# Seven products of halves for the last three spans of an expert layer

## The chip, the cores and the metric

The kernel runs on one core of a Trainium2 chip. The engines named are TensorE (PE, with its weight loads shown as PEld), VectorE (DVE), ScalarE (ACT), GpSimd (POOL) and SyncE (SP, which here only issues DMAs). The metric is the device time of one execution in microseconds. Three runs of the kernel before gave 257.63, 256.58 and 257.5 us, a median of 257.5.

## The reference

The work is block-causal attention (8 batches, 8 heads, 576 positions, 64 columns a head, blocks of 64), whose output becomes the input `x` (4608 tokens, 512 columns) of a layer with two parallel first matrices:

```python
attn = softmax(where(block_i >= block_j, q @ k.T / sqrt(64), -1e9))
x = (attn @ v).transpose(0, 2, 1, 3).reshape(4608, 512)
g = np.maximum(x @ w1, x @ w2)      # w1, w2: 512 x 1024
out = g @ w_out                     # w_out: 1024 x 512, out in fp32
```

## The kernel before

The kernel uses max(a, b) = b + relu(a - b). It forms d = w1 - w2 (`d_sb`) and M = w2 @ w_out (`m_sb`) once. Then h = relu(x @ d) is kept in a tile called `g`, and y = x @ M + h @ w_out. So y has an inner length of 512 + 1024 = 1536, that is 12 chunks of 128: four from `xT` against `m_sb` and eight from `g` against `wo_sb`. All of these are bf16; PSUM and the output are fp32.

The tokens are cut into ten spans (lines 70 to 73 of the kernel): 256, 320, then 512 each, and 448 for the last one. A span starts at token t0, and where t0 is not a multiple of 128 the 64 columns that are left over (`carry`) are copied by POOL from the `g` tile of the span before (L235), so that y always works on whole tiles of 128 tokens. From span 2 on each has four such tiles.

For a span, `h_unit(i, f)` makes one of eight blocks of 128 hidden columns: four matmuls with `d_sb` as the stationary operand and up to 512 tokens as the moving one (L243), and then a relu by VectorE from PSUM into `g` (L248). `y_unit(i, s)` makes one tile of 128 tokens by 512 columns: twelve matmuls 512 wide (L285), a copy by VectorE into a `y` tile (L290), and a store from SP's queue (L291). The last tile of all, `y_last` (L294 on), is cut into pieces of 256, 128 and 128 columns. Their copies are by ScalarE, VectorE and ScalarE (L305), and the last piece is stored from ScalarE's queue (L306).

Each unit is a generator that issues one matmul a step. `plan()` puts the units into a list, in order, each with the number of tokens that must be done before it may start, and a cost. `fill(n)` takes steps of the first unit in the list that may start, and the attention code calls it between its own matmuls, so that PE always has something to do. Attention works on pairs of heads (32 pairs, two a group): scores into PSUM (L399, L417), exp by ScalarE (L423), masks by POOL (L428), then the matmul of the attention values (L507) two pairs later, with a reciprocal and a multiply by VectorE (L513, L514) into `xp`. `xp` becomes columns of `xT` by a DMA transpose (L525), or, for the last group, by 18 transposes on PE and two copies by VectorE (L545 to L551). Within the group loop `pool_work(p)` issues POOL's casts and loads after each pair.

The order on each engine is the order in which the program is written out (a manual schedule); nothing is reordered. Tiles come from pools with few buffers: `ps_m` has four PSUM banks, shared by h, y, the attention values and the transposes; `y` has four SBUF tiles; `w1raw` has four, used only while d is made; `bT_sb` is used only while M is made; `qkn` holds cast q and k.

Since the last batch's tokens count as done only when its last group has been transposed, spans 8 and 9, and what is left of span 7, come after attention:

```python
    x_out(NG - 1)
    done_tokens[0] = old
    fill(NY)
    done_tokens[0] = NTOK
    fill(len(units) * NFF * 12)
```

Of the kernel before, what the change touches and what calls it, by code (L numbers as in the profile page):

```python
# [8 lines left out]
FP32 = mybir.dt.float32  # L9
BF16 = mybir.dt.bfloat16  # L10
AF = mybir.ActivationFunctionType
# [3 lines left out]
def kernel(  # L15
# [10 lines left out]
    nc = tc.nc  # L26

    B, H, S, D = q.shape
    P = 128
# [3 lines left out]
    d_model = H * D  # L33
# [3 lines left out]
    NTOK = B * S  # L37
# [33 lines left out]
    spans = [(0, QCUT), (QCUT, S - QCUT)]  # L71
    spans += [(t0, min(SPAN, NTOK - t0)) for t0 in range(S, NTOK, SPAN)]
    NSPAN = len(spans)


    carry = [t0 % P for t0, _ in spans]
    tiles = [(carry[i] + w) // P for i, (_, w) in enumerate(spans)]

# [5 lines left out]
    wraw = ctx.enter_context(tc.tile_pool(name="wraw", bufs=4))  # L84
    qkn = ctx.enter_context(tc.tile_pool(name="qkn", bufs=2))
    g_pool = ctx.enter_context(tc.tile_pool(name="g", bufs=2))
    y_pool = ctx.enter_context(tc.tile_pool(name="y", bufs=4))
    ps_s = ctx.enter_context(tc.tile_pool(name="ps_s", bufs=2, space=bass.MemoryType.PSUM))
    ps_m = ctx.enter_context(tc.tile_pool(name="ps_m", bufs=4, space=bass.MemoryType.PSUM))

# [9 lines left out]
    xT = ring.tile([P, NDM, NTOK + BLK], BF16, name="xT")  # L100
    d_sb = wpool.tile([P, NDM, d_ff], BF16, name="d_sb")
    bT_sb = wpool.tile([P, NFF, d_model], BF16, name="bT_sb")
    m_sb = wpool.tile([P, NDM, d_model], BF16, name="m_sb")
    wo_sb = wpool.tile([P, NFF, d_model], BF16, name="wo_sb")
# [5 lines left out]
    dve, pool, act = nc.vector.tensor_copy, nc.gpsimd.tensor_copy, nc.scalar.copy  # L110
# [51 lines left out]
    def load_v(b, c):  # L162
        rows = min(P, S - c * P)
        nc.gpsimd.dma_start(  # L164
            out=vv_r[b % NV][P - rows:, c, :, :D],
            in_=v[b, :, c * P:c * P + rows, :].rearrange("h p d -> p h d"),
        )
# [7 lines left out]
    for j in range(d_ff // WB):  # L175
        row, n = (1, j) if j < 3 else (3, 0)
        t0 = 3 * S - 3 * BLK + n * NDM * WB
# [21 lines left out]
    dve, pool, act = nc.vector.tensor_copy, nc.gpsimd.tensor_copy, nc.scalar.copy  # L199
# [28 lines left out]
    g_tiles = {}  # L228

    def h_unit(i, f):  # L230
        if f == 0:
            g_tiles[i] = g_pool.tile([P, NFF, SPAN + BLK], BF16, name="g")
            if carry[i]:
                end = carry[i - 1] + spans[i - 1][1]
                nc.gpsimd.tensor_copy(  # L235
                    out=g_tiles[i][:, :, :carry[i]],
                    in_=g_tiles[i - 1][:, :, end - carry[i]:end])
        g = g_tiles[i]
        t0, w = spans[i]
        m = carry[i]  # L240
        pt = ps_m.tile([P, SPAN], FP32, name="ps_h", tag="m")
        for c in range(NDM):
            nc.tensor.matmul(  # L243
                pt[:, :w], d_sb[:, c, f * P:(f + 1) * P], xT[:, c, t0:t0 + w],
                start=(c == 0), stop=(c == NDM - 1),
            )
            if c == NDM - 1:
                nc.vector.tensor_scalar_max(g[:, f, m:m + w], pt[:, :w], 0.0)  # L248
            yield

    def bT_unit(j):
        pt = ps_m.tile([P, 2, NDM, P], BF16, name="ps_bT", tag="m")
        for i in range(2):
            for c in range(NDM):
                nc.tensor.transpose(pt[:, i, c, :], w2_sb[j][:, c, i * P:(i + 1) * P], ident[:])
                if i == 1 and c == NDM - 1:
                    (act if j % 2 else dve)(
                        out=bT_sb[:, 2 * j:2 * j + 2, :],
                        in_=pt.rearrange("p i c d -> p i (c d)"))
                yield  # L260
# [19 lines left out]
    def y_unit(i, s):  # L280
        t0 = spans[i][0] - carry[i] + s * P
        py = ps_m.tile([P, d_model], FP32, name="ps_y", tag="m")
        terms = y_terms(i, s)
        for n, (lhs, rhs) in enumerate(terms):
            nc.tensor.matmul(  # L285
                py[:], lhs, rhs, start=(n == 0), stop=(n == len(terms) - 1),
            )
            if n == len(terms) - 1:
                y = y_pool.tile([P, d_model], FP32, name="y")
                nc.vector.tensor_copy(out=y[:], in_=py[:])  # L290
                nc.sync.dma_start(out=out[t0:t0 + P, :], in_=y[:])  # L291
            yield

    def y_last(i, s):  # L294
        t0 = spans[i][0] - carry[i] + s * P
        for m, w, copy, queue in ((0, 256, act, SP), (256, P, dve, SP), (384, P, act, ACT)):
            py = ps_m.tile([P, w], FP32, name="ps_y", tag="m")
            terms = y_terms(i, s)
            for n, (lhs, rhs) in enumerate(terms):
                nc.tensor.matmul(  # L300
                    py[:], lhs, rhs[:, m:m + w], start=(n == 0), stop=(n == len(terms) - 1),
                )
                if n == len(terms) - 1:
                    y = y_pool.tile([P, d_model], FP32, name="y")
                    copy(out=y[:, :w], in_=py[:])  # L305
                    queue.dma_start(out=out[t0:t0 + P, m:m + w], in_=y[:, :w])  # L306
                yield


    units = []  # L310
    NY = NDM + NFF

    def plan():
        def h(i, f):
            t0, w = spans[i]
            units.append((h_unit(i, f), t0 + w, w / SPAN, NDM))

        def y(i, s, last=False):
            t0, w = spans[i]
            if last:  # L320
                units.append((y_last(i, s), t0 + w, 0.333, 3 * NY))
            else:
                units.append((y_unit(i, s), t0 + w, 1.0, NY))

        for i in range(NSPAN):
            for f in range(NFF):
                h(i, f)
                if i == 0 and f % 2:
                    units.append((bT_unit(f // 2), 0, 0.25, 2 * NDM))
                if i > 2 and f % 2 == 0 and f // 2 < tiles[i - 1]:  # L330
                    y(i - 1, f // 2)
            if i == 1:
                for n in range(2 * NDM):
                    units.append((m_unit(n // NDM, n % NDM), 0, 0.5, NFF))
                for j in range(2):
                    for s in range(tiles[j]):
                        y(j, s)
        n = tiles[-1]
        for s in range(n):
            y(NSPAN - 1, s, s == n - 1)  # L340

    plan()
    todo = [[n, u, need, cost] for u, need, cost, n in units]
# [225 lines left out]
    def pool_work(s):  # L569
        g, i = divmod(s, 2)  # L570
        if s == 4:
            load_qk(4, (SP, SP), gated=True)
        elif s == 5:
            load_qk(5, (SP, SP), gated=True)
            cast("q", 4, ((pool, 0, RPP),))
            cast("k", 4, ((pool, 0, RPP),))
        else:
            if i == 1 and g + 3 < NG:
                load_qk(g + 3, (SP, SP), gated=True)
            if i == 1 and g + 2 < NG:  # L580
                cast("q", g + 2, ((pool, 0, RPP),))
                cast("k", g + 2, ((pool, 0, RPP),))
            nb, j = divmod(s + 2, HP)
            if nb < B:
                for c in ((0, 1), (2, 3), (4,), ())[j]:
                    load_v(nb, c)
            for nm in "qk":
                if i == 1 and g + 3 < NG and by_dma(nm, g + 3):
                    load_blocks(nm, g + 3)
# [112 lines left out]
    n = fill_of(GPB)  # L702
# [10 lines left out]
    for g in range(GPB + 1, NG):  # L713
        a, b = 2 * g, 2 * g + 1
        old = done_tokens[0]
        if x_due:
            x_out(x_due.pop())
        n, new = fill_of(g), done_tokens[0]
        region(tile_0(a), tile_1(a))
        lo, hi = max(3, n // 18), n * 2 // 9  # L720
        for p, tiles in ((a, lambda: (tile_2(a), tile_0(b))), (b, lambda: (tile_1(b), tile_2(b)))):
            done_tokens[0] = old if p == a and x_by_dma(g - 2) else new
            fill(hi)
            av_with(p - LAG, lo)
            done_tokens[0] = new
            if p % 2 and x_by_dma(g - 1):
                x_dma(g - 1)
            if p % 2 == 0:
                for nm in "qk":
                    if g + 1 < NG and by_dma(nm, g + 1):  # L730
                        transpose_blocks(nm, g + 1)
            copy_out = t_pair(p)
            outs = tiles()
            copy_out()
            region(*outs)
            if p % 2 and g + 1 < NG:
                pad_keys(p + 1)
                pad_keys(p + 2)
            pool_work(p)
        x_due.append(g - 1)  # L740
        fill(n - 2 * (lo + hi))
    for p in range(NPAIR - LAG, NPAIR):
# [48 lines left out]
```

## Time and profile before

| what | value |
|---|---|
| median of three runs | 257.5 us (256.58 to 257.63) |
| the profiled execution: its own time, as the page gives it, is its span | 255.8 us |
| PE busy | 245.8 us, 96% |
| VectorE busy | 149.9 us, 59% |
| ScalarE busy | 120.1 us, 47% |
| POOL busy | 128.0 us, 50% |
| matmuls of y, 512 wide (L285) | 420, with 35 copies and 35 stores of 256 KB |
| matmuls of h (L243) | 320, with 80 relus |
| last matmul of attention values starts, last group | 210.59 us, 24 matmuls |
| first h of span 8 | 218.31 us |
| first matmuls of the last tile | 249.40 us |

A row of the groups reads: line, engine, operation, what it writes and reads, shapes, count, then busy time in us and the mean of one in ns, then the engine's idle time just before such instructions and what ended it. A row of the timeline reads: start in us, duration in us, engine, line, operation, count. Matmuls are pipelined: the duration of one (380 ns for 512 columns) is longer than the distance to the next, so the pitch is read from start to start. A row of the DMA issues ends in the time from issue to landing.

### The profile page before, as it was taken

To read this page: it belongs to the slowest core of one execution; us is meant where nothing else is said; L and a number is where in the kernel's file an instruction comes from. 1 tells how busy PE (TensorE), PEld (TensorE's weight loads), DVE (VectorE), ACT (ScalarE), POOL (GpSimd) and SP (SyncE) were. 2 spreads that over 40 slices of the span, in tenths; PEclk is the share of its full clock that TensorE was granted. 3 is DMA by queue.
4 is the path that set the end of the run, shared out by engine and by line. 5 is a ranking of instruction groups with operands and counts; after the bars stand their busy time and mean duration, and the time that the engine had idled before them with its cause. 6 is when DMAs were issued, how large, how long until landed. Compare 5 with 4: busy or idle time off the path is not lost.

```text
span 255.8 us, 6863 instructions
## 1 busy us (share of the span) xinstructions
PE 245.8 (96%) x2803; PEld 136.5 (53%) x2803; DVE 149.9 (59%) x320; ACT 120.1 (47%) x159; POOL 128.0 (50%) x294
## 2 busy tenths in 40 slices
PE   8699999899999999999999999999999999999994
PEld 2346767765555555555555555555555554444443
DVE  4876986656576447644764476457544864664521
ACT  2788864477565555555555555555555400000000
POOL 1986951588869457845784578557331200000000
PEclk9999999999999999999999999999999999999999
DMA  6999999599999999999999999999952301202122
GB/s 240 316 222 308 190 265 229 191 127 175 171 144 231 154 219 147 214 138 232 161 197 153 218 166 219 151 216 160 118 103 85 85 23 70 85 0 82 66 100 84
DMA packets 104384, 41.29 MB, mean 161 GB/s; under 512 B 89248, under 2 KB 93728, under 8 KB 104352
## 3 DMA queue, kind: packets, MB, share of 16 engines
q0 software_dynamic: 65952, 11.87, 60.9%
q1 hardware_dynamic: 37984, 28.32, 48.4%
q10 hardware_dynamic: 416, 0.66, 0.8%
q8 instruction: 22, 0.36, 0.7%
q14 instruction: 10, 0.08, 0.1%
HBM read 34.60 MB, written 9.44 MB: 172 GB/s over the span
## 4 chain that ended last, share of the span: by engine, by line
PE 86%; DMA 6%; POOL 3%; ACT 2%; DVE 1%; issue 1%; SPq 0%; POOLq 0%
PE ps_y L285 37%; PE ps_h L243 22%; PE ps_o L507 10%; PE ps_s L399 8%; PE ps_w L369 4%; DMA kraw<-in_k_dram 3%; DMA qraw<-in_q_dram 3%; PE ps_qT L380 2%; PE ps_M L266 1%; ACT aT L423 1%; PE ps_y L300 1%; POOL kn L160 1%; PE ps_s L417 1%; POOL wo_sb L196 1%; PE ps_xe L545 1%
## 5 line engine op out<-in xcount | busy, mean ns | idle before, releaser
L423 ACT ACTIVATE aT<-ps_s 128x1024 bf16<-128x1024 f32 (+2 forms) x100 | 95.7, 994 | 46.1 <-PE ps_s L399 34.2
L285 PE MATMUL ps_y<-wo_sb,g 128*128 128x512 bf16 x280 | 70.6, 380 | 0.0
L243 PE MATMUL ps_h<-xT,d_sb 128*128 128x512 bf16 (+3 forms) x320 | 68.3, 358 | 0.3 <-DVE d_sb L190 0.3
L248 DVE TENSOR_SCALAR g<-ps_h 128x512 bf16<-128x512 f32 (+3 forms) x80 | 50.7, 637 | 17.5 <-PE ps_h L243 15.2
L428 POOL MEMSET aT<- 64x128 bf16 x124 | 22.0, 199 | 60.9 <-ACT aT L423 59.8
L290 DVE COPY y<-ps_y 128x512 f32<-128x512 f32 x35 | 24.2, 692 | 45.9 <-PE ps_y L285 45.0
L243 PEld LDWEIGHTS <-d_sb 128*128 128x128 bf16 x320 | 29.5, 98 | 30.1 <-issue 2.3
L507 PEld LDWEIGHTS <-aT 128*128 128x128 bf16 x960 | 37.2, 98 | 13.5 <-issue 0.8
L285 PEld LDWEIGHTS <-g 128*128 128x128 bf16 x280 | 24.9, 98 | 30.7 <-issue 5.3
L507 PE MATMUL ps_o<-vv,aT 128*128 128x65 bf16 x960 | 39.8, 194 | 0.0
L285 PE MATMUL ps_y<-m_sb,xT 128*128 128x512 bf16 x140 | 38.1, 379 | 0.0
L164 POOL DMA_DIRECT2D vv<-in_v_dram x40 | 34.0, 857 | 1.3 <-issue 0.9
L399 PE MATMUL ps_s<-qT,kT 64*128 64x64 bf16 (+6 forms) x344 | 31.2, 280 | 1.6 <-ACT kT L388 0.7
L514 DVE TENSOR_TENSOR xp<-ps_o,rec 128x256 bf16<-128x256 f32 (+1 forms) x64 | 31.4, 491 | 2.2
L137 POOL DMA_DIRECT2D kb<-in_k_dram x40 | 29.4, 759 | 0.0
L513 DVE RECIPROCAL rec<-ps_o 128x4 f32<-128x4 f32 (+1 forms) x64 | 11.9, 186 | 23.7 <-PE ps_o L507 23.5
L305 ACT COPY y<-ps_y 128x256 f32<-128x256 f32 (+1 forms) x2 | 0.6, 318 | 48.4 <-PE ps_y L300 48.4
L388 ACT COPY qT<-ps_qT 128x576 bf16<-128x576 bf16 (+1 forms) x17 | 10.3, 613 | 27.2 <-PE ps_qT L380 27.2
L160 POOL CAST qn<-qraw 128x1152 bf16<-128x1152 f32 (+1 forms) x16 | 17.0, 1061 | 8.4 <-DMA qraw<-in_q_dram 8.4
L285 PEld LDWEIGHTS <-xT 128*128 128x128 bf16 x140 | 12.8, 98 | 13.1 <-issue 0.4
L399 PEld LDWEIGHTS <-kT 64*128 64x128 bf16 x344 | 12.0, 94 | 11.6 <-issue 6.2
L235 POOL COPY g<-g 128x512 bf16<-128x512 bf16 x8 | 4.9, 613 | 22.4 <-DVE g L248 22.1
(58 smaller groups left out, 152.1 us busy)
## 6 DMA issues: line engine op xcount, KB each, us to landing
qraw<-in_q_dram SPq DMA_DIRECT2D x16, 576.0 KB, 4.9
out_dram<-y SPq DMA_DIRECT2D x35, 256.0 KB, 4.1
vv<-in_v_dram POOLq DMA_DIRECT2D x32, 128.0 KB, 5.6
kraw<-in_k_dram SPq DMA_DIRECT2D x5, 576.0 KB, 7.5
kb<-in_k_dram POOLq DMA_DIRECT2D x40, 72.0 KB, 6.4
w1raw<-in_moe_w_dram POOLq DMA_DIRECT2D x4, 512.0 KB, 7.4
xT<-in_moe_w_dram POOLq DMA_DIRECT2D x4, 256.0 KB, 7.9
wo_sb<-in_moe_w_out_dram POOLq DMA_DIRECT2D x2, 512.0 KB, 10.2
```

The costliest lines, as they stand in the source:

```text
L137: nc.gpsimd.dma_start(out=n[h * BLK:(h + 1) * BLK, :, s], in_=(q if nm == "q" else k)[b, 4 * u + 2 * s + h].rearrange("(j p) d -> p j d", ...
L160: copy(out=n[:, j0:j1], in_=t[:, j0:j1])
L164: nc.gpsimd.dma_start(out=vv_r[b % NV][P - rows:, c, :, :D], in_=v[b, :, c * P:c * P + rows, :].rearrange("h p d -> p h d"),)
L243: nc.tensor.matmul(pt[:, :w], d_sb[:, c, f * P:(f + 1) * P], xT[:, c, t0:t0 + w], start=(c == 0), stop=(c == NDM - 1),)
L248: nc.vector.tensor_scalar_max(g[:, f, m:m + w], pt[:, :w], 0.0)
L285: nc.tensor.matmul(py[:], lhs, rhs, start=(n == 0), stop=(n == len(terms) - 1),)
L290: nc.vector.tensor_copy(out=y[:], in_=py[:])
L399: nc.tensor.matmul(ps[:, hh, col:col + w], kT[r, k0:k0 + P], qT[r, q0:q0 + w], start=True, stop=True,)
L423: nc.scalar.activation(out=aT_r[p % NA][:, :, a0:a0 + w], in_=ps[:, :, :w], func=AF.Exp, scale=scale,)
L428: (eng or nc.gpsimd).memset(aT_r[p % NA][BLK:, :, a0:a0 + BLK], 0.0)
L507: nc.tensor.matmul(po[:, gi, hh, :], a[:, hh, a0:a0 + P], vv[:, c, h0 + 2 * hh, :], start=(mm == 0), stop=(mm == n_mm - 1),)
L514: nc.vector.tensor_mul(xp[:, :, ts[0]:ts[0] + n, p % 2].rearrange("q s t d -> q t s d"), po[:, :, :, :D], rec[:, :n].to_broadcast([P, n, 2 ...
```

## The change

For spans 7, 8 and 9 (`FAST = 7`: h with the new relus from span 7 on) the four y units are gone. A span's y is a product of a matrix of 512 tokens by 1536 and one of 1536 by 512. Both are cut into halves in each direction: tokens into two rows of 256, the inner length into two halves of 768 (two chunks of x and four of g each), and the output into two columns of 256. Strassen's scheme in the form of Winograd then takes seven products of halves, not eight, with sums of halves before and sums of products after:

- `weight_sums(n)` makes four sums of the halves of M and w_out once, in bf16, into the four `w1raw` buffers. It is called eight times, after `pool_work(p)` for pairs 10 to 17. Each call is one VectorE instruction (128x512 for M's part, 128x1024 for w_out's).
- `row_sums(i, n, k)` makes four sums of the halves of x (k = 0, 128x512) and of g (k = 1, 128x1024), on VectorE in bf16. Those of x are issued after the relus of blocks 2, 4, 5 and 6 of the span, those of g when products 1 and 6 start. The sums of g lie in `bT_sb`, those of x in the rest of the `w1raw` buffers or in a `qkn` tile.
- `product(i, n)` is a unit of 12 matmuls 256 wide into one PSUM bank (two tiles of 128 tokens beside each other).
- `after(...)` folds a product into fp32 `y` tiles: a copy by ScalarE for product 1, and adds by VectorE, with PSUM and a `y` tile as operands, for the others: seven in all. Four stores a span of 256 tokens by 256 columns go out from SP. The last product is cut in three, with three adds and three small stores, all from SP's queue.
- The relus of spans 8 and 9, and those of the odd blocks of span 7, are on ScalarE.
- `y` has six buffers.
- In the list, product n of span i-1 stands after block f of span i (order 1, 2, 6, 5, 4, 7, 3); those of span 9 come last (order 1, 4, 6, 5, 7, 3, 2).

The x sums of the last x tokens, the adds and the stores are all in order on their engines, as everything else is.

```diff
+    FAST = 7
-    y_pool = ctx.enter_context(tc.tile_pool(name="y", bufs=4))
+    y_pool = ctx.enter_context(tc.tile_pool(name="y", bufs=6))
...
-                nc.vector.tensor_scalar_max(g[:, f, m:m + w], pt[:, :w], 0.0)
+                if i >= FAST and on_act(i, f):
+                    nc.scalar.activation(out=g[:, f, m:m + w], in_=pt[:, :w], func=AF.Relu)
+                else:
+                    nc.vector.tensor_scalar_max(g[:, f, m:m + w], pt[:, :w], 0.0)
+                if i >= FAST and f in X_SUMS:
+                    row_sums(i, X_SUMS[f], 0)
...
+    def s_parts(i, n):
+        if i % 2 and ("x", n) not in slot:
+            t = qkn.tile([P, 4, HN], BF16, name="xsum", tag="kn")
+            slot["x", n], slot["x", n + 1] = t[:, 0:2], t[:, 2:4]
+        return (slot["x", n] if i % 2 else slot[n][:, 6:8],
+                bT_sb[:, 2 * n - 2:2 * n].rearrange("p a (b c) -> p (a b) c", c=HN))
+
+    def weight_sums(n):
+        m, op, x, y = (
+            (1, sub, (0, 1), (0, 0)), (3, sub, (1, 1), (0, 1)),
+            (2, add, 3, (0, 0)), (4, sub, (1, 0), 2))[n // 2]
+        if not slot:
+            for k in range(1, 5):
+                slot[k] = wraw.tile([P, 8, HN], BF16, name="sums", tag="w1raw")
+        get = lambda z: b_parts(*z) if isinstance(z, tuple) else t_parts(z)
+        op(t_parts(m)[n % 2], get(x)[n % 2], get(y)[n % 2])
+
+    def row_sums(i, n, k):
+        op, x, y = (
+            (add, (1, 0), (1, 1)), (sub, 1, (0, 0)), (sub, (0, 0), (1, 0)), (sub, (0, 1), 2))[n - 1]
+        get = lambda z: a_parts(i, *z) if isinstance(z, tuple) else s_parts(i, z)
+        op(s_parts(i, n)[k], get(x)[k], get(y)[k])
...
+    G_SUMS = {1: (1, 2), 6: (4, 3)}
+    X_SUMS = {2: 1, 4: 2, 5: 3, 6: 4}
+
+    def on_act(i, f):
+        return i >= 8 or f % 2
+
+    def product(i, n, cuts=((0, 0, HN), (1, 0, HN))):
+        for m in G_SUMS.get(n, ()):
+            row_sums(i, m, 1)
...
+            for c in range(6):
+                nc.tensor.matmul(
+                    pt[:, q0:q0 + w], lhs[c][:, s * P:(s + 1) * P], rhs[c][:, m:m + w],
+                    start=(c == 0 and q0 == 0), stop=(c == 5 and q0 + w == pt.shape[1]),
+                )
+                if c == 5 and q0 + w == pt.shape[1]:
+                    after(i, n, st, pt, p0, q0 + w)
+                yield
...
+        if n == 1:
+            st["u"] = new()
+            act(out=st["u"][:], in_=pt[:])
+        elif n == 2:
+            if i < NSPAN - 1:
+                st["c"] = new()
+                add(st["c"][:], pt[:], st["u"][:])
+            else:
+                add(st["c"][:, p0:p0 + w], pt[:], st["c"][:, p0:p0 + w])
+            store(st["c"], 0, 0)
+        elif n == 6 and i < NSPAN - 1:
+            add(st["u"][:], pt[:], st["u"][:])
+        elif n == 6:
+            st["c"], st["u"] = st["u"], new()
+            add(st["u"][:], pt[:], st["c"][:])
+        elif n == 5:
+            st["v"] = new()
+            add(st["v"][:], pt[:], st["u"][:])
+            if 4 in st:
+                add(st["u"][:], st[4][:], st["u"][:])
+        elif n == 4:
+            if "v" in st:
+                add(st["u"][:], pt[:], st["u"][:])
+            st[4] = pt
+        elif n == 7:
+            t = new()
+            add(t[:], pt[:], st["v"][:])
+            store(t, 1, 1)
+            add(st["u"][:], pt[:], st["u"][:])
+            store(st["u"], 1, 0)
+        elif n == 3:
+            add(st["v"][:], pt[:], st["v"][:])
+            store(st["v"], 0, 1)
+
+    ORDER = (1, 2, 6, 5, 4, 7, 3)
+    LAST = (1, 4, 6, 5, 7, 3, 2)
...
+                if i > FAST and f < 7:
+                    units.append((product(i - 1, ORDER[f]), spans[i - 1][0] + spans[i - 1][1], 0.5, NY))
...
-                if i > 2 and f % 2 == 0 and f // 2 < tiles[i - 1]:
+                if 2 < i <= FAST and f % 2 == 0 and f // 2 < tiles[i - 1]:
                     y(i - 1, f // 2)
...
-        n = tiles[-1]
-        for s in range(n):
-            y(NSPAN - 1, s, s == n - 1)
+        for n in LAST:
+            units.append((product(NSPAN - 1, n, ((0, 0, HN), (1, 0, P), (1, P, P))) if n == 2 else
+                          product(NSPAN - 1, n), NTOK, 0.5, 18 if n == 2 else NY))
...
             pool_work(p)
+            if 0 <= p - 10 < 8:
+                weight_sums(p - 10)
```

More of the change, by code (lines that the diff above doesn't have):

```diff
@@ L307, in y_last, with a_parts, b_parts @@
                 yield
+    HN = d_model // 2
+    slot, part_sums = {}, {}
+    sub, add = nc.vector.tensor_sub, nc.vector.tensor_add
+    def a_parts(i, row, half):
+        g, t0 = g_tiles[i], spans[i][0] - carry[i] + 2 * row * P
+        return (xT[:, 2 * half:2 * half + 2, t0:t0 + 2 * P],
+                g[:, 4 * half:4 * half + 4, 2 * row * P:2 * row * P + 2 * P])
+    def b_parts(half, col):
+        cs = slice(col * HN, (col + 1) * HN)
+        return m_sb[:, 2 * half:2 * half + 2, cs], wo_sb[:, 4 * half:4 * half + 4, cs]
@@ new lines, in t_parts @@
+    def t_parts(n):
+        return slot[n][:, 0:2], slot[n][:, 2:6]
+    def s_parts(i, n):
[13 more added lines that the diff above has]
+        op(t_parts(m)[n % 2], get(x)[n % 2], get(y)[n % 2])
@@ new lines, in row_sums, with chunks @@
+    def row_sums(i, n, k):
[3 more added lines that the diff above has]
+        op(s_parts(i, n)[k], get(x)[k], get(y)[k])
+    def chunks(parts):
+        return [p[:, c] for p in parts for c in range(p.shape[1])]
+    NP7 = 7
+    G_SUMS = {1: (1, 2), 6: (4, 3)}
+    X_SUMS = {2: 1, 4: 2, 5: 3, 6: 4}
+    def on_act(i, f):
+        return i >= 8 or f % 2
@@ new lines, in product @@
+    def product(i, n, cuts=((0, 0, HN), (1, 0, HN))):
+        for m in G_SUMS.get(n, ()):
+            row_sums(i, m, 1)
+        lhs = chunks({1: lambda: a_parts(i, 0, 0), 2: lambda: a_parts(i, 0, 1), 4: lambda: a_parts(i, 1, 1)}.get(
+            n, lambda: s_parts(i, {3: 4, 5: 1, 6: 2, 7: 3}[n]))())
+        rhs = chunks({1: lambda: b_parts(0, 0), 2: lambda: b_parts(1, 0), 3: lambda: b_parts(1, 1)}.get(
+            n, lambda: t_parts({4: 4, 5: 1, 6: 2, 7: 3}[n]))())
+        st = part_sums.setdefault(i, {})
+        pt = None
+        for k, (s, m, w) in enumerate(cuts):
+            if pt is None or len(cuts) > 2:
+                pt, p0 = ps_m.tile([P, 2 * HN if len(cuts) == 2 else w], FP32, name="ps_p", tag="m"), s * HN + m
+            q0 = s * HN + m - p0
+            for c in range(6):
[6 more added lines that the diff above has]
+                yield
@@ new lines, in after, with store @@
+    def after(i, n, st, pt, p0, w):
+        new = lambda: y_pool.tile([P, d_model], FP32, name="y")
+        t0 = spans[i][0] - carry[i]
+        def store(t, row, col):
+            r0 = t0 + 2 * row * P
+            if w < d_model:
+                s, m = divmod(p0, HN)
+                nc.sync.dma_start(
+                    out=out[r0 + s * P:r0 + (s + 1) * P, col * HN + m:col * HN + m + w], in_=t[:, p0:p0 + w])
+                return
+            nc.sync.dma_start(
+                out=out[r0:r0 + 2 * P, col * HN:(col + 1) * HN].rearrange("(s p) d -> p s d", p=P),
+                in_=t.rearrange("p (s d) -> p s d", s=2))
+        if n == 1:
[31 more added lines that the diff above has]
+            store(st["v"], 0, 1)
```

## The prediction

> **What bounds the kernel now.** I read the page's engine shares, the clock row and the chain of waits first, then the timeline of the tail (from the last attention pair on, 205 us), then the shapes of the VectorE and ScalarE groups, then the landing times of the stores.
>
> ```profile
> PE 245.8 (96%) x2803; PEld 136.5 (53%) x2803; DVE 149.9 (59%) x320; ACT 120.1 (47%) x159; POOL 128.0 (50%) x294
> ...
> PEclk9999999999999999999999999999999999999999
> ...
> PE ps_y L285 37%; PE ps_h L243 22%; PE ps_o L507 10%; PE ps_s L399 8%; PE ps_w L369 4%; DMA kraw<-in_k_dram 3%; DMA qraw<-in_q_dram 3%; PE ps_qT L380 2%; PE ps_M L266 1%; ACT aT L423 1%; PE ps_y L300 1%; POOL kn L160 1%; PE ps_s L417 1%; POOL wo_sb L196 1%; PE ps_xe L545 1%
> ```
>
> PE is busy all through, at a full granted clock, and y (L285) is the largest share of the chain. So fewer columns streamed for y come straight off the end, as long as PE is never made to wait.
>
> ```profile
> 218.31 7.83 PE L243 MATMUL ps_h<-xT,d_sb 128*128 128x512 bf16 x36
> ...
> 244.22 1.03 PE L285 MATMUL ps_y<-m_sb,xT 128*128 128x512 bf16 x4
> ...
> 246.81 1.03 PE L285 MATMUL ps_y<-m_sb,xT 128*128 128x512 bf16 x4
> 247.01 0.69 DVE L290 COPY y<-ps_y 128x512 f32<-128x512 f32 x1 [1.90 <-PE ps_y L285]
> ...
> 249.40 0.60 PE L300 MATMUL ps_y<-m_sb,xT 128*128 128x256 bf16 x4
> ...
> 250.71 0.39 PE L300 MATMUL ps_y<-m_sb,xT 128*128 128x128 bf16 x4
> ...
> 251.38 0.39 PE L300 MATMUL ps_y<-m_sb,xT 128*128 128x128 bf16 x4
> ...
> 252.25 0.27 ACT L305 COPY y<-ps_y 128x128 f32<-128x128 f32 x1 [0.97 <-PE ps_y L300]
> 252.54 0.36 ACTq L306 DMA_DIRECT2D out_dram<-y  x1
> ```
>
> Starts give the pitch. A y unit of 12 matmuls 512 wide takes 246.81 - 244.22 = 2.59 us (216 ns each). The 12 matmuls 256 wide of the last tile take 250.71 - 249.40 = 1.31 us (109 ns each), each with its own weight load, and 12 of 128 take 0.67 us (56 ns). A PE result is picked up about 0.20 us after the next unit starts (246.81 to 247.01). The whole tail holds no PE wait of note.
>
> ```profile
> L290 DVE COPY y<-ps_y 128x512 f32<-128x512 f32 x35 | 24.2, 692 | 45.9 <-PE ps_y L285 45.0
> L514 DVE TENSOR_TENSOR xp<-ps_o,rec 128x384 bf16<-128x384 f32 x32 | 17.8, 557 | 1.1
> L514 DVE TENSOR_TENSOR xp<-ps_o,rec 128x256 bf16<-128x256 f32 x32 | 13.6, 424 | 1.1
> L190 DVE TENSOR_TENSOR d_sb<-w1raw,xT 128x1024 bf16<-128x1024 f32 x4 | 4.9, 1215 | 0.0
> L257 DVE COPY bT_sb<-ps_bT 128x1024 bf16<-128x1024 bf16 x2 | 1.4, 682 | 0.0
> L551 DVE COPY xT<-ps_xo 128x512 bf16<-128x512 bf16 x3 | 1.2, 415 | 0.0
> ```
>
> These price VectorE: 1.04 ns per fp32 column, about half that where both sides are two-byte.
>
> **The change, part by part.** The page gives the profiled execution a span of 255.8 us; the three runs have a median of 257.5. The sum is made on the span, and I take 1.7 us around it as unchanged.
>
> *Products for units (gain).* A span has four y units, 4 x 2.59 = 10.36 us. Seven products of 12 matmuls 256 wide are 7 x 1.31 = 9.17. That is 1.19 less for each of spans 7 and 8. The last span took 252.05 - 241.63 = 10.42 (249.40 + 1.31 + 2 x 0.67 is the 252.05) and takes 6 x 1.31 + 0.655 + 2 x 0.335 = 9.19, so 1.23 less. Sum 3.61 us.
>
> *Sums of weights.* Eight VectorE sums, four 128x512 and four 128x1024, all bf16 in SBUF, one after each pair from 10 to 17 (about 70 to 115 us). No row has a bf16 sum of two SBUF operands. Bounds: the two-byte copies (415 and 682 ns) and the fp32 rate (690 by the L514 slope, and 1215). I take the first, because two-byte rows halve the column time here. The Trainium skill's page "VectorE: DVE Perf Modes" (section "The perf-mode tier table") lists a bf16 sum of two operands at 2x, 1224 ns for 2048 columns; by that, my estimate is some 0.42 and 0.69 us, and no run here shows it. The sums delay only what is behind them on VectorE. After a qT copy in every second group comes a run without a gap:
>
> ```profile
> 94.87 0.75 DVE L388 COPY qT<-ps_qT 128x576 bf16<-128x576 bf16 x1
> 95.75 0.69 DVE L290 COPY y<-ps_y 128x512 f32<-128x512 f32 x1
> 96.69 0.69 DVE L248 TENSOR_SCALAR g<-ps_h 128x512 bf16<-128x512 f32 x1 [0.24 <-POOL aT L428]
> ```
>
> There 0.42 us pushes y, the relu and the next reciprocal by 0.2 to 0.4 us, and PE has a bank or two in hand. The other six sums fall before idle times of 0.7 to 1.6 us. Cost 0.2 us, bounds 0 and 1.4 (two runs late by 0.69 with no spare bank).
>
> A rule speaks against these sums. First the row that bears on it:
>
> ```profile
> 26.46 1.22 DVE L190 TENSOR_TENSOR d_sb<-w1raw,xT 128x1024 bf16<-128x1024 f32 x1
> ...
> 26.94 1.13 POOL L406 COPY kz<-kT 128x128 bf16<-128x128 bf16 x2
> ```
>
> The two POOL copies, beside a VectorE difference of two SBUF tensors, took 1.13 us together, where the pair at 41.51 took 0.52. The Trainium skill's page "SBUF — State Buffer" (section "Who interferes with whom") says that a VectorE operation with two SBUF inputs and a GpSimd operation that reads SBUF exclude each other. By it, my estimate is that each weight sum could wait for up to one POOL operation, 1.15 us for a cast, eight of them for 9 us if all met one and all counted. By the row it was POOL that waited, some 0.6 us, and VectorE kept its 1215. In the order of the changed program only the carry copy of g (0.61 us) and the kz copies come near, off the chain, so I add nothing.
>
> *Relus on ScalarE.* An exp of 384 columns takes 498 ns, one of 768 815 ns, so 512 come to about 0.60 us and 448 to 0.55, under the 0.864 us of an h unit (and the 0.757 of a 448-wide one). The built program has one table load, as before. In span 7 the four odd ones stand among the last exps: that of f=1 falls into the 1.98 us that ScalarE idles before 201.21, f=3 ends near 204.0, and its bank is wanted at 204.7. Cost 0; if the exps ran late, PE would wait here for a bank, 0.6 us at most.
>
> *Row sums and adds on VectorE.* A span gains four x sums (0.42), four g sums (0.68) and seven adds of a PSUM product and an fp32 y tile (512 columns: 692 ns by L290, 690 by the L514 slope); it loses four copies and, in the last two, eight relus. The places where PE waits for VectorE, walked with these durations in the built order:
> - Span 7. PE is where it was at 205.80. Products 1, 2, 6 and 5 and half of product 4 stand between attention values (24 matmuls 0.72 us, 6 of them 0.18), and the half ends at 213.32. The next 18 transposes need the last xp. VectorE reaches it late: sums 1 and 2 206.66 to 208.04, reciprocal and xp to 208.8, c 209.34 to 210.03, sums 4 and 3 to 211.41, reciprocal and xp to 212.0, u to 212.69, reciprocal and xp to 213.45. PE waits 0.15 to 0.2 us. Then transposes 0.40, half a product 0.655, products 7 and 3: h of span 8 starts at 217.20, not 218.31. The gain there is 1.11 instead of 1.19: cost 0.08.
> - Span 8. h 217.20 to 224.86 with the first h of span 9, then seven times a product and an h, 7 x 2.07, to 239.34. VectorE has about 9.3 us of work in these 14.5, and every bank is free in time. Cost 0. Its queue has nothing behind it but these adds.
> - Span 9. Sums 1 and 2 follow the last relu and end near 241.5; product 6 wants them at 242.0. PE ends at 239.34 + 9.19 = 248.53. VectorE is nearly full: add of product 5 to 245.47, u to 246.19, after product 7 two adds to 246.91 and 247.63, product 3 to 248.35, the three pieces of product 2 (0.43, 0.29, 0.29) to 249.45. Before, the last eviction ended 0.47 us after PE's 252.05; now 0.92 after 248.53. Cost 0.45.
>
> *Stores.* SP issues them in order (0.33 us each); 256 KB go out as 1 KB rows, the last one on SP instead of ACT's queue.
>
> ```profile
> out_dram<-y SPq DMA_DIRECT2D x1, 64.0 KB, 1.6
> out_dram<-y ACTq DMA_DIRECT2D x1, 64.0 KB, 2.2
> ```
>
> Landing 1.6 for 2.2 gains up to 0.6, but three 256 KB stores are issued from 246.9 on within 1.5 us and may push it by 0.4 (full stores landed in 2.0 us here, alone; at the 266 GB/s seen at 70% share one is 0.7 us of the engines). Gain 0.2, bounds -0.6 and +0.6. The six y buffers come free in time: the latest need is that of the store at 237.5, landed by 240, at 244.8.
>
> Sum: 3.61 - 0.2 - 0.08 - 0.45 + 0.2 = 3.08 off. Span 252.7, time 254.4 us.
>
> **Rivals.**
> 1. *The bf16 sums run at the fp32 rate* (690 and 1215 ns). For it: the only sum of two SBUF tensors here, L190, has that rate. Against: one of its inputs is fp32. The last xp of attention then ends at 215.45, so PE loses 2.0 us at the transposes; in the last span product 6 waits 0.4 us for sum 2 and the last add ends at 252.25 against 252.52 before. With the store's 0.2 and some 0.3 for the weight sums nothing is left: 257.3 us, no change.
> 2. *The adds of PSUM and fp32 SBUF cost double*, 1.38 us. For it: the second operand of L514 is only a repeated reciprocal, so no row reads two full tensors of fp32 from both memories. Against: L514 and L290 have the same rate per column, one operand or two. In span 7 the transposes come 1.4 us late and h units 2 and 3 of span 8 wait for banks, 2.9 us together; in span 9 a queue of adds trails PE and the last ends at 253.8, 4.3 later. 7.2 - 3.1: 261.6 us, slower. It decides from about 1.0 us an add, 0.3 over my price (3.1 / 7.2 x 0.69).
> 3. *The products do not stream faster*, because a weight load (98 ns, PEld) per 109 ns leaves no slack in long runs. Break-even is 10.36 / 84 = 123 ns a matmul. Against: 12 in a row kept 109 and 24 of 128 columns kept 56. At 115 ns 1.5 us of the gain go (84 x 6 ns x 3): 255.9.
>
> **How the numbers follow.** Forecast 0.70 (own range 253.5 to 255.4: weight sums 0 to 0.6, store -0.6 to +0.6); rival 3 and small stalls together, 255.4 to 256.2, 0.10; rival 1, 0.12; rival 2, 0.08. About 0.5% (1.3 us) can be told from no change here, since the three runs span 256.58 to 257.63. So faster 0.80, same 0.12, slower 0.08. The range reaches from 253.3 to rival 1 with 0.3 on top, 257.6.
>
> **What would show it.** After: matmuls of L386 with starts 109 ns apart and 1.31 us a product; PE busy 242 us of a span near 252.7; h of span 8 near 217.2; sums of 128x1024 at about 0.68 and adds at 0.69 us; weight sums with no PE idle behind them; last eviction some 0.9 us after the last matmul, and last landing under 2.2 us. I am wrong if a sum or add costs over 1 us, if the transposes of the last x wait over 0.5 us, or if PE shows gaps at 70 to 115 us.

## The result: 1.4% faster, inside the range

The changed kernel took 254.07 us in the median of four runs (253.27 to 254.91), beside 257.56 (256.58 to 258.09) before: a ratio of 0.9862, 95% interval 0.9825 to 0.9899. The forecast was 254.4 us. The span of the profiled execution fell from 255.8 to 252.7 us, where the sum had 252.7; the four runs after had spans of 251.5 to 253.1.

The page of the changed kernel, busy times and the chain:

```profile
PE 242.5 (96%) x2893; PEld 145.9 (58%) x2893; DVE 158.7 (63%) x343; ACT 132.6 (52%) x180; POOL 129.1 (51%) x294
...
PE ps_y L291 26%; PE ps_h L244 22%; PE ps_p L386 11%; PE ps_o L644 10%; PE ps_s L536 8%; PE ps_w L506 4%; DMA kraw<-in_k_dram 4%; DMA qraw<-in_q_dram 2%; PE ps_qT L517 2%; PE ps_M L272 1%; ACT aT L560 1%; POOL kn L161 1%; PE ps_s L554 1%; POOL wo_sb L197 1%; PE ps_xe L682 1%
```

PE is still the bound, 3.3 us less busy for 3.1 us of span. y and the products together are 37% of the chain's span, where y had 38% with its last tile.

The timeline of the changed kernel from the last attention pair on (start in us, duration, engine, line):

```profile
205.70 0.34 PE L644 MATMUL ps_o<-vv,aT 128*128 128x65 bf16 x6
...
212.88 0.56 DVE L651 TENSOR_TENSOR xp<-ps_o,rec 128x384 bf16<-128x384 f32 x1
...
213.21 0.60 PE L386 MATMUL ps_p<-sums,g 128*128 128x256 bf16 x4
...
217.42 7.83 PE L244 MATMUL ps_h<-xT,d_sb 128*128 128x512 bf16 x36
...
239.55 0.38 PE L386 MATMUL ps_p<-m_sb,xT 128*128 128x256 bf16 x2
...
240.86 0.38 PE L386 MATMUL ps_p<-sums,xT 128*128 128x256 bf16 x2
...
242.17 0.38 PE L386 MATMUL ps_p<-sums,xsum 128*128 128x256 bf16 x2
...
248.40 0.28 PE L386 MATMUL ps_p<-m_sb,xT 128*128 128x128 bf16 x2
```

A product takes 1.31 us (239.55, 240.86, 242.17), the price that the last tile of the kernel before had shown, and nothing stands between them. The last xp of attention (212.88 + 0.56 = 213.44) is done before the half of product 4 ends (213.21 + 4 x 0.109 = 213.65), so the transposes do not wait for it.

Two places in the code can be matched between any two of these kernels and serve as marks: the six matmuls of attention values at 66.95 and at 205.40 us before. In the kernel before they are 138.45 us apart, and after 205.70 - 67.25 = 138.45 too. So everything between 67 and 205 us, weight sums included, costs the same, and what differs ahead of 67 us is how the execution started (0.3 us later here). The tail, from that mark to the end, took 255.8 - 205.40 = 50.4 us before and 252.7 - 205.70 = 47.0 after. The tail is compared in the experiments too, because a start differs by more than most of the effects.

VectorE and ScalarE groups of the changed kernel, by shape:

```profile
L360 DVE TENSOR_TENSOR bT_sb<-g 128x1024 bf16<-128x1024 bf16 x6 | 4.1, 688 | 6.1 <-ACT g L250 6.0
...
L360 DVE TENSOR_TENSOR bT_sb<-bT_sb,g 128x1024 bf16<-128x1024 bf16 x3 | 2.5, 838 | 0.3
L440 DVE TENSOR_TENSOR y<-ps_p,y 128x512 f32<-128x512 f32 x3 | 2.1, 691 | 0.5 <-PE ps_p L386 0.4
...
L360 DVE TENSOR_TENSOR xsum<-xT 128x512 bf16<-128x512 bf16 x4 | 1.7, 416 | 0.0
...
L354 DVE TENSOR_TENSOR sums<-wo_sb 128x1024 bf16<-128x1024 bf16 x2 | 1.4, 682 | 0.0
```

The two prices that no row had shown are settled: a bf16 sum of two SBUF tensors is 0.42 us for 512 columns and 0.68 to 0.69 for 1024 (the mean of 838 is told at the end), and an add of PSUM and fp32 SBUF 0.69 for 512. From 416 and 682 ns a sum costs 0.52 ns a column more, which drawn on to 2048 columns makes 1.21 us, an estimate. The Trainium skill's page "VectorE: DVE Perf Modes" (section "The perf-mode tier table") lists 1224 ns for a bf16 sum of two operands of 2048 columns, which agrees.

### The profile page after: what moved, and what is told of

Its sections match the earlier page's. It is cut to its first block, busy times and chain, and to the rows that moved or that the text cites. A ratio compares the mean times of both kernels' runs of the same rounds, so it can differ in the third digit from the quotient of the medians.

```text
span 252.7 us, 7097 instructions
## 1 busy us (share of the span) xinstructions
PE 242.5 (96%) x2893; PEld 145.9 (58%) x2893; DVE 158.7 (63%) x343; ACT 132.6 (52%) x180; POOL 129.1 (51%) x294
## 4 chain that ended last, share of the span: by engine, by line
PE 86%; DMA 6%; POOL 3%; ACT 2%; DVE 1%; issue 1%; SPq 0%; POOLq 0%
PE ps_y L291 26%; PE ps_h L244 22%; PE ps_p L386 11%; PE ps_o L644 10%; PE ps_s L536 8%; PE ps_w L506 4%; DMA kraw<-in_k_dram 4%; DMA qraw<-in_q_dram 2%; PE ps_qT L517 2%; PE ps_M L272 1%; ACT aT L560 1%; POOL kn L161 1%; PE ps_s L554 1%; POOL wo_sb L197 1%; PE ps_xe L682 1%
## 5 line engine op out<-in xcount | busy, mean ns | idle before, releaser
L291 PE MATMUL ps_y<-wo_sb,g 128*128 128x512 bf16 x192 | 49.7, 380 | 0.0
L252 DVE TENSOR_SCALAR g<-ps_h 128x512 bf16<-128x512 f32 (+2 forms) x60 | 37.4, 627 | 14.3 <-PE ps_h L244 12.7
L296 DVE COPY y<-ps_y 128x512 f32<-128x512 f32 x24 | 16.6, 691 | 25.6 <-PE ps_y L291 19.9
L291 PEld LDWEIGHTS <-g 128*128 128x128 bf16 x192 | 16.5, 98 | 20.9 <-issue 5.3
L291 PE MATMUL ps_y<-m_sb,xT 128*128 128x512 bf16 x96 | 26.5, 379 | 0.0
L250 ACT ACTIVATE g<-ps_h 128x512 bf16<-128x512 f32 (+1 forms) x20 | 11.5, 576 | 22.3 <-PE ps_h L244 22.3
L236 POOL COPY g<-g 128x512 bf16<-128x512 bf16 x8 | 5.9, 734 | 20.6 <-ACT g L250 20.3
L291 PEld LDWEIGHTS <-xT 128*128 128x128 bf16 x96 | 8.5, 98 | 8.6 <-issue 0.4
```

Of the source, the lines that this page charges most:

```text
L291: nc.tensor.matmul(py[:], lhs, rhs, start=(n == 0), stop=(n == len(terms) - 1),)
```

## The experiments

**The change once more, and its two halves alone.** Theory A: the gain is streamed columns of y, and all else is hidden. First the same kernel again, with no edit.

> The changed kernel once more, as the measure for the other runs. Theory A (the gain is streamed columns of y, all else is hidden): 254.1 us, span 252.7 with the first h of span 8 near 217.1 to 217.5. The start up to 20 us differs by some 0.3 us from run to run if the 0.3 us that the profile after lost there is chance; if it belongs to the change, it is there again.

253.53 us beside 257.06, ratio 0.9859 (0.9832 to 0.9886), span 251.8.

```profile
66.37 0.34 PE L644 MATMUL ps_o<-vv,aT 128*128 128x65 bf16 x6
...
204.82 0.34 PE L644 MATMUL ps_o<-vv,aT 128*128 128x65 bf16 x6
```

Between the marks it is 138.45 us again, and from the second to the end 47.0 again. Only the first mark moved, by 0.9 us: the start is chance, and the tail is not.

All relus back on VectorE:

```diff
     def on_act(i, f):
-        return i >= 8 or f % 2
+        return False
```

> All relus on VectorE, products as in the change. Theory A: VectorE has four relus more (0.6 us each) before the last transposes, which wait 0.5 to 1.5 us; spans 8 and 9 still fit. 254.6 to 255.6 us. Rival B (moving relus to ScalarE is what brings the gain): 256.5 or more. Rival C (VectorE has slack everywhere): 254.1.

253.39 us, ratio 0.9865 (0.9825 to 0.9905). My expectation of 0.5 to 1.5 us lost fell, and rival C holds for this edit. Its timeline at the last transposes:

```profile
212.02 0.56 DVE L651 TENSOR_TENSOR xp<-ps_o,rec 128x384 bf16<-128x384 f32 x1
212.14 0.60 PE L386 MATMUL ps_p<-sums,g 128*128 128x256 bf16 x4
...
212.68 0.20 PE L682 MATMUL ps_xe<-ident,xp 64*128 64x64 bf16 x1
```

The last xp ends at 212.58 and PE is done with its half product at 212.14 + 0.44 = 212.58: the extra relus have eaten the margin and nothing more. So the relus on ScalarE bring no measurable time.

The relus alone, without products, in the kernel before:

```diff
-                nc.vector.tensor_scalar_max(g[:, f, m:m + w], pt[:, :w], 0.0)
+                if i >= 8 or (i == 7 and f % 2):
+                    nc.scalar.activation(out=g[:, f, m:m + w], in_=pt[:, :w], func=AF.Relu)
+                else:
+                    nc.vector.tensor_scalar_max(g[:, f, m:m + w], pt[:, :w], 0.0)
```

> The kernel before with nothing changed but the relus of spans 8 and 9, and the odd ones of span 7, on ScalarE. Theory A: no PE wait was there to remove, so no change, 257.5 us. Rival B: some 1 us or more faster.

257.12 us, ratio 1.0000 (0.9966 to 1.0033). No change, as theory A has it; rival B is out.

The width alone: y of the last three spans from matmuls of 256 columns, with all eight products' columns and no sums.

```diff
+        cuts = ((0, 256), (256, 256)) if i >= 7 else ((0, d_model),)
         for n, (lhs, rhs) in enumerate(terms):
-            nc.tensor.matmul(
-                py[:], lhs, rhs, start=(n == 0), stop=(n == len(terms) - 1),
-            )
+            for c0, cw in cuts:
+                nc.tensor.matmul(
+                    py[:, c0:c0 + cw], lhs, rhs[:, c0:c0 + cw],
+                    start=(n == 0 and c0 == 0), stop=(n == len(terms) - 1 and c0 + cw == d_model),
+                )
```

> The kernel before with each y matmul of the last three spans, except the last tile, cut into two of 256 columns: all eight products' columns, no sums. Theory A (109 ns for 256 columns, 216 for 512): 11 tiles x 12 x 2.4 ns = 0.3 us slower, 257.9 us. Rival D (long runs of 256 pay for weight loads, 115 ns or more): 1.8 us slower or more. Rival E (256 columns stream faster than half of 512 and this is part of the gain): faster than 257.5.

257.75 us, ratio 1.0021 (0.9995 to 1.0047): between no change and 1.2 us slower. That is theory A's 0.3 us within what can be told, and it excludes rival D's 1.8 us, and most of rival E. The pitch in its trace, at a granted clock of 1.00 in this stretch, settles the rest:

```profile
244.51 1.04 PE L287 MATMUL ps_y<-m_sb,xT 128*128 128x256 bf16 x8
...
247.13 1.04 PE L287 MATMUL ps_y<-m_sb,xT 128*128 128x256 bf16 x8
```

A y unit of 24 matmuls 256 wide takes 247.13 - 244.51 = 2.62 us (109 ns each), where 12 of 512 took 2.59: 0.03 us more for each of eleven units, which is theory A's 0.3. Narrower matmuls are not faster, so rival E is out too. So the gain is in the eighth product that is left out, not in the narrower matmuls.

**How much room VectorE has.** Row sums of span 7 used again for spans 8 and 9, so that the output of those is not y:

```diff
     def row_sums(i, n, k):
+        if i > FAST:
+            return
...
-        if i % 2 and ("x", n) not in slot:
+        if ("x", n) not in slot:
...
-        return (slot["x", n] if i % 2 else slot[n][:, 6:8],
+        return (slot["x", n],
```

> The sums of x and g are made for span 7 alone, and spans 8 and 9 use those of span 7 again (16 VectorE sums left out; the output of spans 8 and 9 is not y). Theory A: they were hidden, 254.0 to 254.1 us, and h of span 8 at the same place. Rival F (the sums hold up products 6 and 5 or the adds behind them): 0.5 to 2 us faster.

253.34 us, ratio 0.9846 (0.9814 to 0.9877), and from the mark (204.63) to the end of the span (251.6) 47.0 us, as with the sums. Sixteen sums cost nothing; rival F is out.

Every sum of x and g twice:

```diff
-        op(s_parts(i, n)[k], get(x)[k], get(y)[k])
+        for _ in range(2):
+            op(s_parts(i, n)[k], get(x)[k], get(y)[k])
```

> Every sum of x and g is issued twice, with the same output, 4 us more of VectorE in each span: the load of rival 1 of the prediction. Theory A with the walk of the prediction: the last xp of attention comes some 2 us late, the transposes wait for it, and in the last span product 6 waits 0.4 us; 256 to 257 us. Rival C (VectorE has slack everywhere): 254.1.

258.24 us, ratio 1.0043 (1.0016 to 1.0070): slower than the kernel before. Its timeline, with what PE waited for in brackets:

```profile
211.37 0.61 PE L387 MATMUL ps_p<-sums,bT_sb 128*128 128x256 bf16 x4 [0.64 <-DVE bT_sb L361]
...
215.87 0.39 PE L387 MATMUL ps_p<-sums,xT 128*128 128x256 bf16 x2 [1.18 <-DVE xp L652]
...
217.16 0.20 PE L685 MATMUL ps_xo<-ident,xp 64*128 64x64 bf16 x1 [0.33 <-DVE xp L652]
...
246.72 0.61 PE L387 MATMUL ps_p<-sums,bT_sb 128*128 128x256 bf16 x4 [0.77 <-DVE bT_sb L361]
```

From the mark (206.41) to the end it is 51.4 us, 4.4 more than in the change. The places are those of the walk in the prediction (product 6 waits for sum 2, attention's last values and transposes wait for xp, product 6 of span 9 waits for its sum), and two of the three waits in span 7 are for xp. Of the 4.4 us, 2.7 lie between the mark and the first h of span 8 (14.40 us for 11.72), none in span 8, 1.1 in the products of span 9 and 0.6 behind PE's end. The expected 256 to 257 was too little. The expectation also calls this the load of rival 1, which it is not: rival 1's prices would add 4 x 0.275 + 4 x 0.533 = 3.2 us a span, the doubling adds 4.4. So there is slack for what was added and not for twice the sums; rival C, slack everywhere, falls here.

The weight sums twice:

```diff
-        op(t_parts(m)[n % 2], get(x)[n % 2], get(y)[n % 2])
+        for _ in range(2):
+            op(t_parts(m)[n % 2], get(x)[n % 2], get(y)[n % 2])
```

> Every sum of weights is issued twice, 4.4 us more of VectorE between 70 and 115 us. Theory A: no PE gap there, 254.1 us. Rival G (they cost 0.2 us as the prediction has it, or more): 254.3 to 255.

253.91 us, ratio 0.9880 (0.9850 to 0.9910). The marks:

```profile
66.85 0.34 PE L645 MATMUL ps_o<-vv,aT 128*128 128x65 bf16 x6
...
205.31 0.34 PE L645 MATMUL ps_o<-vv,aT 128*128 128x65 bf16 x6
```

138.46 us between them, 0.01 more than in the kernel before, which has none. Rival G is out: the weight sums are free, even doubled.

**More spans.** If columns of y are all that counts, an earlier span should bring 1.19 us as well. Span 6 too:

```diff
-    FAST = 7
+    FAST = 6
```

> Four spans instead of three have seven products. Span 6 is worked off beside the last attention groups. Theory A: 1.19 us more off, 252.9 us. Rival H (beside attention VectorE has too little room: some 4 us more work in the last 25 us before 205): less than half of it, 253.6 to 254.5.

252.99 us, ratio 0.9829 (0.9798 to 0.9860). Its profile says where a part of the 1.19 us went:

```profile
184.43 1.02 ACT L560 ACTIVATE aT<-ps_s 128x1024 bf16<-128x1024 f32 x1
...
185.35 0.58 ACT L411 COPY y<-ps_p 128x512 f32<-128x512 f32 x1
...
185.98 0.90 PE L644 MATMUL ps_o<-vv,aT 128*128 128x65 bf16 x24 [0.40 <-ACT y L411]
```

From the mark at 172.48 to that at 204.25 it is 31.77 us, where the change once more has 204.82 - 172.42 = 32.40: 0.63 gained of 1.19, which is neither theory A's whole nor less than half, as rival H had it. The wait that the trace shows is for ScalarE, not for VectorE: the copy of product 1 stands behind an exp and holds a PSUM bank that the attention values want. Four kernels with that copy on VectorE ahead of span 7, and with `FAST` 6, 5, 4 and 3:

```diff
-            act(out=st["u"][:], in_=pt[:])
+            (dve if i < 7 else act)(out=st["u"][:], in_=pt[:])
```

> Four spans have seven products; the copy of product 1 of span 6 is on VectorE, not behind the exps on ScalarE, where the run with four spans lost 0.4 to 0.6 us of its 1.19. Theory A: 1.19 us off against three spans, ratio to before 0.981. Rival I (another wait beside attention takes its place): 0.984, as with the copy on ScalarE.

> Five spans, copies of spans 5 and 6 on VectorE. Theory A: 2.4 us off against three spans, ratio 0.977. Rival H (VectorE beside attention is too full): no better than four spans.

> Six spans. Theory A: 3.6 us off against three spans, ratio 0.972. Rival H: no better than five.

> Seven spans; the products of span 3 start some 5 us after the last weight sum. Theory A: 4.8 us off against three spans, ratio 0.967. Rival H: no better than six, or a new wait on the weight sums.

| spans with seven products | median us | ratio to before (95%) |
|---|---|---|
| 4 (`FAST` 6) | 252.48 | 0.9821 (0.9796 to 0.9846) |
| 5 | 251.88 | 0.9792 (0.9768 to 0.9816) |
| 6 | 251.03 | 0.9763 (0.9738 to 0.9787) |
| 7 (`FAST` 3) | 250.29 | 0.9738 (0.9714 to 0.9762) |

With four spans the step is whole. From the mark at 172.42 to the last one, first the change once more and then this kernel:

```profile
172.42 0.35 PE L644 MATMUL ps_o<-vv,aT 128*128 128x65 bf16 x6
...
204.82 0.34 PE L644 MATMUL ps_o<-vv,aT 128*128 128x65 bf16 x6
```

```profile
172.42 0.35 PE L644 MATMUL ps_o<-vv,aT 128*128 128x65 bf16 x6
...
203.63 0.34 PE L644 MATMUL ps_o<-vv,aT 128*128 128x65 bf16 x6
```

204.82 - 203.63 = 1.19 us, the price of a span to the hundredth, so rival I is out there, and the copy's place on ScalarE is shown to be what the run before lost. Each span ahead of that brings less. The intervals of neighbours in the table overlap, so the marks are taken: from the first to the last it is 137.26 us with four spans, then 136.51, 135.75 and 134.99. That is 0.75 or 0.76 us a span, more than rival H's nothing and less than theory A's 1.19. In the kernel with five spans the rest is a wait for VectorE:

```profile
168.08 0.68 DVE L437 TENSOR_TENSOR y<-ps_p,y 128x512 f32<-128x512 f32 x1
...
168.89 0.42 DVE L651 TENSOR_TENSOR xp<-ps_o,rec 128x256 bf16<-128x256 f32 x1
168.93 0.20 PE L517 MATMUL ps_qT<-ident,qn 64*128 64x64 bf16 x1
...
169.37 0.43 PE L517 MATMUL ps_qT<-ident,qn 64*128 64x64 bf16 x17 [0.24 <-DVE xp L651]
```

The second add of product 7 stands ahead of attention's xp, whose bank the transposes of q want. The first of the 18 transposes starts at 168.93 and the others at 169.37, 0.44 us later. The attention values at 167.28 are followed by the next such six matmuls 4.67 us later there, and 4.22 in the change. The kernels with six and seven spans show this wait two and three times. In the kernel with four spans the last transposes of q are over at 182.4, ten us before the adds of product 7 of span 6 (192.65), and it shows no such wait. No run moved the add behind xp, so that the order is the cause is read from the trace, not tested. The version with seven spans beats the change: 250.29 us beside 253.53 for the change in another comparison, ratios to before 0.9738 and 0.9859 with intervals that do not meet.

## Why the prediction was right, point by point

| step, us off the span | predicted | measured | from |
|---|---|---|---|
| products, span 7, with the wait at the transposes | 1.11 | 1.19 | mark to first h of span 8: 12.91, then 11.72 |
| products, spans 8 and 9 | 2.42 | 2.43 | first h of span 8 to PE's end: 33.74, then 31.31 |
| weight sums | -0.2 | 0.00 | 138.45 us between marks in both |
| last evictions behind PE | -0.45 | -0.03 | 0.47, then 0.50 (249.23 - 248.73) |
| stores | +0.2 | -0.19 | last eviction to end: 3.28, then 3.47 |
| start, up to 67 us | 0 | -0.30 | first mark 66.95, then 67.25 |
| sum | 3.08 | 3.10 | |

The measured rows split the 3.1 us between the two profiled spans, so their sum is that by construction; the spans are known to 0.1 us.

- *Products for units.* Right in mechanism and size: 109 ns a matmul held through the tail, and 1.19 us a span came out to the hundredth in span 6 too. The wait of 0.08 us that the walk had at the last transposes was not there. Rival 3 is excluded by the pitch. The six `y` buffers were not tried alone; the columns account for the gain without them.
- *Sums and adds on VectorE.* The prices were right, so rivals 1 and 2 have no ground: 0.68 and not 1.22 us, 0.69 and not 1.38. That VectorE's room would have decided was right too, as doubling the sums showed. Whether rival 1's 2.9 us of loss was sized right is not shown, since no run has sums at its prices.
- *Weight sums.* The term was 0.2 us, the cost nothing. The step "pushes y, the relu and the next reciprocal by 0.2 to 0.4 us" hardly happened: counted from the first mark, y's copy came 0.12 us later (96.17 - 67.25 = 28.92, and 95.75 - 66.95 = 28.80 before), and the relu (29.74) and the reciprocal (30.34) came when they had come before. The sum fell into short gaps that VectorE had there anyway, such as the 0.24 us ahead of the relu.
- *The queue of adds at the end.* This term was mis-sized, 0.45 for 0.03 us. The walk put the last adds end to end, 0.72 us apart. Neither the second nor the third of the three rows of 512 columns below uses what the add just ahead of it writes, and the trace starts them closer:

```profile
245.72 0.69 DVE L428 TENSOR_TENSOR y<-ps_p,y 128x512 f32<-128x512 f32 x1
...
246.33 0.68 DVE L435 TENSOR_TENSOR y<-ps_p,y 128x512 f32<-128x512 f32 x1
...
246.93 0.68 DVE L437 TENSOR_TENSOR y<-ps_p,y 128x512 f32<-128x512 f32 x1
...
248.27 0.96 DVE L417 TENSOR_TENSOR y<-ps_p,y 128x256 f32<-128x256 f32 x3
...
248.51 0.39 PE L386 MATMUL ps_p<-wo_sb,g 128*128 128x128 bf16 x4
```

They are 0.60 to 0.61 us apart at 0.69 of duration. So the last eviction ends at 248.27 + 0.96 = 249.23, 0.50 us after PE's 248.51 + 4 x 0.056 = 248.73. The same made room for the relus on VectorE: in that run the twenty VectorE operations from 203.07 us to the end of the last xp at 212.58 last 10.2 us added up, and took 9.5.
- *Stores.* The sign was wrong, +0.2 for -0.19. The prediction took 0.33 us for each issue from SP but charged no wait for it:

```profile
248.81 1.43 SPq L402 DMA_DIRECT2D out_dram<-y  x3
```

The three small stores take 1.43 us to issue, so the last one, whose add ends at 249.23, is issued at 249.85 (248.81 + 1.43 - 0.39), 0.6 us later. Before, ScalarE's queue issued it 0.02 us after the copy. The landings took 2.3, 2.0 and 1.8 us, so the last one gained 0.4 on the 2.2 of before, and the issue lost more than that. Three 256 KB stores stand ahead of them and took 2.3 to 2.5 us, and the DMA engines were full. The end of the changed kernel, then the busiest half microsecond of the end before (PE, PEld, DVE, ACT, POOL busy, clock, DMA share, GB/s):

```profile
249.00:250.00 1.00, 0.00 (x0) 0.00 (x0) 0.23 (x1) 0.00 (x0) 0.00 (x0) 1.00 1.02 343
250.00:251.00 1.00, 0.00 (x0) 0.00 (x0) 0.00 (x0) 0.00 (x0) 0.00 (x0) 1.00 1.00 315
```

```profile
251.00:251.50 0.50, 0.50 (x13) 0.50 (x11) 0.00 (x0) 0.28 (x1) 0.00 (x0) 1.00 0.70 266
```

Three terms were mis-sized: the queue of adds (0.42 us too dear), the weight sums (0.2 too dear) and the stores (0.39 too cheap). With the late start they happened to cancel, and that is luck, so the hundredths of agreement in the span mean nothing; the 3.6 us of the first two rows do.

## What to carry to other kernels

Where one engine's stream is the bound and its rate at another shape can be read from starts in the trace, fewer columns come off the end one for one, as long as the other engines' new work finds a gap or a spare bank. Count that room where the bound engine waits, not in busy shares: VectorE was busy for 63% of the span, and twice the sums cost 4.4 us. Look for adds that nobody waits for ahead of a small operation that PE waits for: beside attention 0.45 us a span was lost at such a place, and to turn the order round is the first thing to try, which no run here did. To compare two kernels to a tenth of a microsecond, measure from a mark in the code that both share, not from the start.

## What the runs showed of the hardware

- A VectorE operation that does not use what the one ahead of it writes can start before that one ends. The adds above start 0.60 us apart while each lasts 0.69, so a walk with durations overstates a queue of them by 14%. Three rows of the changed kernel beside attention show both cases:

```profile
97.59 0.17 DVE L650 RECIPROCAL rec<-ps_o 128x4 f32<-128x4 f32 x1
...
97.80 0.42 DVE L651 TENSOR_TENSOR xp<-ps_o,rec 128x256 bf16<-128x256 f32 x1
...
98.14 0.68 DVE L252 TENSOR_SCALAR g<-ps_h 128x512 bf16<-128x512 f32 x1
```

The multiply reads the reciprocal and starts 0.04 us after its end. The relu reads neither and starts 0.08 us before the end of the multiply.
- VectorE sums and POOL copies held each other up. In the changed kernel:

```profile
206.93 0.69 DVE L360 TENSOR_TENSOR bT_sb<-g 128x1024 bf16<-128x1024 bf16 x1
...
207.02 1.08 POOL L236 COPY g<-g 128x512 bf16<-128x512 bf16 x1 [3.17 <-ACT g L250]
...
207.72 0.91 DVE L360 TENSOR_TENSOR bT_sb<-bT_sb,g 128x1024 bf16<-128x1024 bf16 x1
```

The POOL copy took 1.08 us, where it took 0.61 without sums beside it, and the second sum 0.91 for 0.69. It is the sums that do it: in the run that makes them for span 7 alone, the copy for span 8, beside sums, keeps its 1.08 us, and the copy for span 9, beside none, takes 0.61.

```profile
205.95 1.08 POOL L236 COPY g<-g 128x512 bf16<-128x512 bf16 x1 [3.17 <-ACT g L250]
224.17 0.61 POOL L236 COPY g<-g 128x512 bf16<-128x512 bf16 x1 [17.15 <-ACT g L250]
```

The Trainium skill's page "SBUF — State Buffer" (section "Who interferes with whom") says that a VectorE operation with two SBUF inputs contends with a GpSimd operation that reads SBUF, over a pair of ports that one of them holds alone. The slowing agrees with that. That each waits for the whole of the other is not shown: sum, copy and sum took 1.70 us together (206.93 to 208.63), where their own prices add up to 1.99. The prediction had expected VectorE to keep its price and only POOL to wait; VectorE lost 0.22 us, and no PE wait came of it.
- A start differs from execution to execution by up to 1.8 us (the first mark lay between 66.18 and 67.96 us in the traces of thirteen of these kernels, which issue the same instructions up to there), more than most of the effects studied here.
